# A VectorE loop and a finer up projection in a cached-attention decode kernel

## The chip, the cores and the metric

The kernel runs on one core of a Trainium2 chip, as one launch. The metric is the device time of that launch in microseconds. Data lie in the chip's HBM (DRAM) before and after; five engines work on them in the core's SBUF and PSUM: TensorE (PE, matmuls into PSUM), VectorE (DVE), ScalarE (ACT), GpSimd (POOL) and SyncE (SP, here only an issuer of DMAs). Each engine has a program of its own, and semaphores order them.

## The reference

One token of each of 8 sequences goes through a gated mix of attention over a long cache and a two-layer MLP. The output is 8 x 1 x 576.

```python
# x: 8 x 1 x 576   k_cache, v_cache: 8 x 32 x 4096 x 128   (bfloat16)
g = sigmoid((x * gate_w).sum(-1, keepdims=True))

q = (x @ wq).reshape(B, 1, 32, 128).transpose(0, 2, 1, 3)
scores = einsum("bhqd,bhkd->bhqk", q, k_cache) * 128 ** -0.5
o = einsum("bhqk,bhkd->bhqd", softmax(scores), v_cache)
a = o.transpose(0, 2, 1, 3).reshape(B, 1, 4096) @ wo

h = gelu(einsum("bsd,df->bsf", layernorm(x), w1) + b1)   # 576 -> 4608
b = einsum("bsf,fd->bsd", h, w2) + b2                    # 4608 -> 576

out = g * a + (1 - g) * b
```

The two caches hold 537 MB, the four weight matrices some 20 MB.

## The kernel before, in words

**Groups.** The attention is cut into 32 groups (`NG`), each of 8 heads (`HB`) of one sequence: `n = 8 * hg + b`. A group's cache is spread over 128 partitions, 16 partitions to a head and 256 keys (`NTT`) to a partition. Its keys come as two halves of 4 MiB into `KB[0]` and `KB[1]`, its values as 8 MiB into `VB`. All three buffers are single: a key half of the next group is loaded when the last multiply has read the old half, the next values when the last P·V matmul has read `VB`.

**One group.** `scores(n)` goes through 8 chunks (`NC`) of 32 keys. In `mult`, VectorE multiplies a chunk with the query (line 413, into one of two halves of `p1`), and TensorE sums groups of eight of the 128 products with an identity as held weights (lines 424 and 169, eight matmuls). In `reduce` (L431) VectorE adds the remaining 16. `softmax(n)` takes the maximum by transposes (L448 to L456), ScalarE does Exp (L457), and VectorE spreads the weights into `P` (L460) and sums them (L463, L464). `total` (L481) sums over partitions, `pv` does 64 matmuls of `P` with `VB` (L474), `evict` copies the result by ScalarE (L486), `gather` (L491) brings the heads together, and `norm` of group n, which stands in group n+1's program behind chunk 1, divides (L497, L498) and writes a column of `OT_sb`. The query is read from `q_bc`, which holds it for all groups, broadcast over partitions (L405).

**Loads.** All large loads are issued by SP in program order (helper lines L283 for keys, L288 for values, L250 for the rest) and share one hardware queue: for each group its two key halves and then its values, each held by a wait for its buffer. The buffer `RB` holds wq, then w1, then w2, then wo; each is loaded when the last matmul on the one before is done.

**The MLP between the groups.** `between(c)` is called behind each chunk and adds other work there. The up projection is 36 blocks of 6 matmuls (`up_proj`, L511), the activation is `act_h`, the down projection 36 blocks of 4 matmuls (`down_proj`, L536). Before, with `u` the key half that is being read:

```python
UP0, UPN = 3, 3          # up projection in key halves 3, 4, 5 (groups 1, 2, 2), 12 blocks in each
DN = 4                   # down projection in group 4
AP = 30                  # output projection of head group hg, from group 30 on
L0, L1 = 5, 29           # the loop's groups: 5 to 28
```

`load_w2` and `load_b2` (four small loads on ScalarE's queue) stand behind group 2, `load_wo` behind group 4.

**Programs.** `Stream` records the operations of each engine with their waits and numbers those that someone waits for. TensorE's program has a loop: `S.marks` holds where each of its groups 5 to 28 begins, and `emit_loop` writes one turn, in which a semaphore is awaited against a register that holds `turn * step + base` (L127). The other four engines' programs are straight code for all groups. A turn can be written once only if all its operations have the same operands in every group; VectorE's did not, since it read the query of group n from a place in `q_bc` and wrote a column of `OT_sb` that both depend on n.

**The end.** Groups 30 and 31 are in straight code in all programs. The last group's values come in parts (`V_LAST`), partly into `KB[0]`, its P·V is done the other way round (`pv_turned`), and `a_proj` and the last sum end the kernel.

Of the kernel before, what the change touches and what calls it, by code (L numbers as in the profile page):

```python
# [20 lines left out]
NJ = F // 128  # L21
# [20 lines left out]
class Stream:  # L42


    def __init__(self, nc):
        self.nc = nc
        self.ops = {e: [] for e in ("sync", "gpsimd", "scalar", "vector", "tensor")}
        self.sem = {e: nc.alloc_semaphore(f"sem_{e}") for e in ("gpsimd", "scalar", "vector", "tensor")}
        self.count = {e: 0 for e in self.sem}
        self.marks = []  # L50

    def op(self, engine, fn, waits=(), dma=None):

# [6 lines left out]
    def resolve(self):  # L60
        used = set()
        for ops in self.ops.values():
            for rec in ops:
                for w in rec[1]:
                    if w[0] == "op":
                        used.add(id(w[2]))
        for e, ops in self.ops.items():
            for rec in ops:
                if id(rec) in used:
                    self.count[e] += 1  # L70
                    rec[2] = self.count[e]
# [24 lines left out]

    def emit_loop(self, engine, eng, seen):

        turns = [self.ops[engine][a:b] for a, b in zip(self.marks[:-1], self.marks[1:])]
        assert len({len(t) for t in turns}) == 1  # L100
        step, waits = {}, []
        for recs in zip(*turns):
            assert len({(r[2] is None, r[3] is None) for r in recs}) == 1
            needs = [self.needs(r) for r in recs]
            assert len({frozenset(n) for n in needs}) == 1
            kept = []
            for key, (sem, val) in needs[0].items():
                vals = [n[key][1] for n in needs]
                d = vals[1] - vals[0]
                assert all(b - a == d for a, b in zip(vals[:-1], vals[1:]))  # L110
                if d == 0:
                    assert seen.get(key, 0) >= val
                    continue
                assert d > 0 and step.setdefault(key, d) == d
                kept.append((key, sem, val))
            waits.append(kept)
        base = {}
        for kept in waits:
            for key, sem, val in kept:
                base[key] = min(base.get(key, val), val)  # L120
        with eng.bass.Fori(0, len(turns), engines=OrderedEngineSet([eng.engine]), head_slot={eng.engine: 0}) as k:
            at = {key: eng.snap(k * step[key] + base[key]) for key in base}
            had = {}
            for rec, kept in zip(turns[0], waits):
                for key, sem, val in kept:
                    if had.get(key, 0) < val:
                        eng.wait_ge(sem, at[key] + (val - base[key]))  # L127
                        had[key] = val
                self.put(engine, eng, rec)
        for key, val in had.items():  # L130
            seen[key] = max(seen.get(key, 0), val + step[key] * (len(turns) - 1))


def bass_gated_mix__mha_block_cached__mixer_channel_mlp__decode_kernel(
# [20 lines left out]
    def pstride(t):  # L155
        return t[tuple([slice(None)] * len(t.shape))].ap[0][0]
# [71 lines left out]
    E = sb("E", [128, NTT], BF16)  # L228
    P = sb("P", [128, NTQ, HB, TQ], BF16)
    es = sb("es", [128, 1], F32)  # L230
    rs = sb("rs", [128, HB], F32)
    O_sb = sb("O_sb", [128, TQ, DH], F32)
    rz = sb("rz", [128, HB], F32)
# [165 lines left out]
    def q_of(b):  # L399
# [4 lines left out]
                start=True, stop=True), [*a_Q, c_Sel, a_qb.get(b - 1)] if i == 0 else ())  # L404
        a_qb[b] = op("scalar", lambda e: e.activation(out=q_bc[:, b, :], in_=qb_ps[:, :], func=ACT.Copy), [t])  # L405

    def mult(n, c):
        hg, b = divmod(n, B)
        u, par = n * NKH + c // NCK, c % 2
        t0 = (c % NCK) * CT  # L410
        qb = bass.AP(tensor=q_bc, offset=q_bc[:, b, hg * DH:(hg + 1) * DH].offset,
                     ap=[[pstride(q_bc), 128], [0, CT], [1, DH]])
        v_mult[n, c] = op("vector", lambda e: e.tensor_tensor(  # L413
            out=p1[:, par, :, :], in0=KB[u % NKH][:, t0:t0 + CT, :], in1=qb, op=ALU.mult),
            [k_land[u], a_qb[b], p_sum.get((n, c - 2) if c >= 2 else (n - 1, c + NC - 2))]
            + ([v_yT, p_yT, p_Q] if n == 0 and c < 2 else []))
        if c % NCK == NCK - 1:
            k_done[u] = v_mult[n, c]
        for i in range(NCH):
            r = bass.AP(tensor=p1, offset=p1[:, par, 0, i * CH:i * CH + 1].offset,  # L420
                        ap=[[pstride(p1), 128], [DH, CT], [1, CH]])
            w = [v_mult[n, c], v_red.get((n, c - 2) if c >= 2 else (n - 1, c + NC - 2)), *a_Q] if i == 0 else ()
            if i == 0:
                fn = lambda e, r=r: e.matmul(tr_ps[par][:, :], lhsT=ident[:, :], rhs=r, start=True, stop=False)  # L424
            else:
                fn = lambda e, r=r, i=i: held(e, tr_ps[par][:, :], ident[:, :], r, i == NCH - 1)
            p_sum[n, c] = op("tensor", fn, w)
# [65 lines left out]
                [a_ev[n], v_norm.get(n - 1), c_selO] if tt == 0 else ())  # L493

    def norm(n):
        hg, b = divmod(n, B)
        t = op("vector", lambda e: e.reciprocal(out=rz[:, :], in_=oz_ps[:, HB:2 * HB]), [p_oz[n]])  # L497
        v_norm[n] = op("vector", lambda e: e.tensor_tensor(  # L498
            out=OT_sb[:, hg * HB:(hg + 1) * HB, b], in0=oz_ps[:, 0:HB], in1=rz[:, :], op=ALU.mult), [t])


    st = {}
# [59 lines left out]
    def a_proj(hg):  # L562
        for h in range(hg * HB, (hg + 1) * HB):
            st["p_a"] = quarters(OT_sb[:, h, :], wo_sb[:, h, :], h == 0, h == H - 1,
                                 [v_norm[hg * B + B - 1], st["ld_wo"], st["v_bx"]] if h == hg * HB else ())


    def pv_turned(n, parts):
# [14 lines left out]
            [p_oz[n], v_rz[n]])  # L583


    UP0, UPN = 3, 3
    DN = 4
    AP = 30
    L0, L1 = 5, 29
    done_a = [0]  # L590
    last = NG - 1
    q_of(0)
    for n in range(NG):
        if L0 <= n <= L1:
            S.marks.append(len(S.ops["tensor"]))

        def between(c, n=n):
            u = n * NKH + c // NCK
            c4 = c % NCK
            if c == 1 and 1 <= n < last:  # L600
                norm(n - 1)
            if n == last and c == NCK:
                load_v_part(n, KB[0], 0, 0, NTK, [k_done[NKH * n]])
                t0 = NTK
                for nt in V_LAST:
                    load_v_part(n, VB, t0 - NTK, t0, t0 + nt, [p_pv[n - 1]])
                    t0 += nt
            if c4 == 2:
                if UP0 <= u < UP0 + UPN:
                    up_proj((u - UP0) * NJ // UPN, (u - UP0 + 1) * NJ // UPN)  # L610
                if n == DN:
                    down_proj((c // NCK) * NJ // 2, (c // NCK + 1) * NJ // 2)
                if n >= AP and done_a[0] < NHG - 1:
                    a_proj(done_a[0])
                    done_a[0] += 1
            if c4 == 3:
                if u == UP0 + UPN - 1:
                    act_h()
                if n == DN and c > NCK:
                    b_out()  # L620
            if n == 0 and c + 1 < B:
                q_of(c + 1)

        scores(n, between)
        softmax(n)
        if n < last:
            total(n)
        if n < last - 1:
            load_k(NKH * (n + 1))
            load_k(NKH * (n + 1) + 1)  # L630
            pv(n, (0,))
            evict(n)
            gather(n)
            if n + 1 < last - 1:
                load_v(n + 1)
        if n == last - 2:
            load_v_part(last - 1, VB, 0, 0, NTK, [v_done[n]])
        if n == last - 1:
            load_k(NKH * last)
            load_k(NKH * last + 1)  # L640
            load_v_part(n, VB, NTK, NTK, NTT, [v_done[n - 1]])
            pv(n, (0,))
        if n * NKH <= UP0 + UPN - 1 <= n * NKH + 1:
            load_w2()
            load_b2()
        if n == DN:
            load_wo()
# [19 lines left out]

    S.resolve()

    def tensor(eng):  # L670
        seen = {}
        S.emit("tensor", eng, seen, 0, S.marks[0])
        S.emit_loop("tensor", eng, seen)
        S.emit("tensor", eng, seen, S.marks[-1])

    with nc.Block() as block:
        for name in ("sync", "gpsimd", "scalar", "vector"):
            getattr(block, name)(lambda eng, name=name: S.emit(name, eng, {}))
        block.tensor(tensor)


# [26 lines left out]
```

## Time and profile before

| | |
|---|---|
| time, median of 3 runs | 1315.97 us (1313.71 to 1316.01) |
| the profiled execution's own time | 1315.18 us |
| its span, first to last instruction | 1313.4 us |
| mean granted TensorE clock | 0.838 |
| VectorE busy | 856.8 us (65%) |
| TensorE busy | 815.9 us (62%) |
| ScalarE busy | 47.9 us (4%) |
| read from HBM | 556.96 MB, 424 GB/s over the span |
| share of the 16 DMA engines' span, data queue q1 | 98.7% |
| chain that ended last | DMA 64%, VectorE 21%, TensorE 13% |

Views used below: the page (its lines on rates, queues and DMA issues), the chain of waits in order of time (start, length, what), the timeline of single engines (start, length, engine, line, operation, and in brackets the idle time before it with what ended it), and windows (busy time of each engine in a stretch, then the granted clock, the DMA engines' mean busy share and GB/s; a share can come out above 1 in a short window). A queue's row gives kind, packets, MB and the time of its packets as a share of 16 engines' span.

### The profile page before, as it was taken

To read this page: it belongs to the slowest core of one execution; us is meant where nothing else is said; L and a number is where in the kernel's file an instruction comes from. 1 tells how busy PE (TensorE), PEld (TensorE's weight loads), DVE (VectorE), ACT (ScalarE), POOL (GpSimd) and SP (SyncE) were. 2 spreads that over 40 slices of the span, in tenths; PEclk is the share of its full clock that TensorE was granted. 3 is DMA by queue.
4 is the path that set the end of the run, shared out by engine and by line. 5 is a ranking of instruction groups with operands and counts; after the bars stand their busy time and mean duration, and the time that the engine had idled before them with its cause. 6 is when DMAs were issued, how large, how long until landed. Compare 5 with 4: busy or idle time off the path is not lost.

```text
span 1313.4 us, 10207 instructions
## 1 busy us (share of the span) xinstructions
PE 815.9 (62%) x5156; PEld 170.7 (13%) x3364; DVE 856.8 (65%) x1094; ACT 47.9 (4%) x81; POOL 1.6 (0%) x12
## 2 busy tenths in 40 slices
PE   3647765655666666666565666565666666666666
PEld 0103311110111100111110111110111110011113
DVE  4565574556666677666677666668665667766685
ACT  1100000000000000000000000000000000000000
POOL 0000000000000000000000000000000000000000
PEclk8867797887887888787888878888977888878788
DMA  9999989999999999999999999999999999999997
GB/s 400 426 437 442 392 357 442 432 408 446 423 441 418 432 431 432 442 431 439 420 431 434 443 425 439 420 433 433 433 444 423 439 422 431 433 444 428 425 403 292
DMA packets 20904, 557.28 MB, mean 424 GB/s; under 512 B 2048, under 2 KB 6160, under 8 KB 7056
## 3 DMA queue, kind: packets, MB, share of 16 engines
q1 hardware_dynamic: 20624, 556.95, 98.7%
q8 instruction: 13, 0.21, 0.1%
q14 instruction: 11, 0.09, 0.0%
q10 hardware_dynamic: 256, 0.03, 0.0%
HBM read 556.96 MB, written 0.01 MB: 424 GB/s over the span
## 4 chain that ended last, share of the span: by engine, by line
DMA 64%; DVE 21%; PE 13%; issue 0%; SPq 0%; ACT 0%
DMA KB<-in_A_k_cache_dram 63%; DVE p L413 17%; PE psb L169 8%; DVE s_sb L431 4%; DMA VB<-in_A_v_cache_dram 2%; PE psb L424 2%; PE psb L511 1%; PE psb L474 1%; SPq L250 0%; DVE P L460 0%; PE psb L491 0%; PE psb L481 0%; ACT E L457 0%; DVE mA L448 0%; ACT O_sb L486 0%
## 5 line engine op out<-in xcount | busy, mean ns | idle before, releaser
L413 DVE TENSOR_TENSOR p<-KB,q_bc 128x4096 bf16<-128x4096 bf16 x256 | 581.9, 2283 | 310.3 <-DMA KB<-in_A_k_cache_dram 310.3
L169 PE MATMUL psb<-p,ident 128*128 128x512 bf16 x1792 | 487.8, 418 | 0.0
L424 PE MATMUL psb<-p,ident 128*128 128x512 bf16 x256 | 111.6, 436 | 299.2 <-DVE p L413 298.8
L431 DVE TENSOR_REDUCE s_sb<-psb 128x32 f32<-128x512 f32 x256 | 175.6, 686 | 91.8 <-PE psb L169 91.6
L474 PE MATMUL psb<-VB,P 128*32 128x512 bf16 x1984 | 176.5, 534 | 0.3 <-DMA VB<-in_A_v_cache_dram 0.2
L424 PEld LDWEIGHTS psb<-p,ident 128*128 128x128 bf16 x256 | 26.4, 103 | 738.9 <-DVE p L413 651.2
L481 PE MATMUL psb<-rs,ones 128*128 128x8 f32 x64 | 18.8, 367 | 155.5 <-DVE rs L464 154.9
L474 PEld LDWEIGHTS psb<-VB,P 128*32 128x32 bf16 x1984 | 64.5, 129 | 98.7 <-issue 83.1
L460 DVE TENSOR_SCALAR P<-E,own 128x256 bf16<-128x256 bf16 x248 | 51.5, 283 | 17.9 <-ACT E L457 17.9
L457 ACT ACTIVATE E<-s_sb,mD 128x256 bf16<-128x256 f32 x32 | 16.2, 507 | 919.5 <-DVE mD L456 919.5
L491 PE MATMUL psb<-selO,O_sb 128*128 128x8 f32 x248 | 33.6, 262 | 21.2 <-ACT O_sb L486 21.2
L481 PEld LDWEIGHTS psb<-rs,ones 128*128 128x128 f32 x64 | 15.8, 307 | 214.9 <-DVE rs L464 214.3
L491 PEld LDWEIGHTS psb<-selO,O_sb 128*128 128x128 f32 x248 | 30.8, 195 | 36.1 <-ACT O_sb L486 36.1
L486 ACT ACTIVATE O_sb<-psb 128x512 f32<-128x512 f32 x31 | 18.5, 596 | 259.0 <-PE psb L474 259.0
L511 PE MATMUL psb<-yT_sb,RB 128*128 128x8 bf16 (+1 forms) x216 | 19.6, 229 | 0.0
L511 PEld LDWEIGHTS psb<-yT_sb,RB 128*128 128x128 bf16 (+1 forms) x216 | 18.6, 165 | 5.7 <-issue 4.3
L448 DVE TENSOR_REDUCE mA<-s_sb 128x1 f32<-128x256 f32 x32 | 13.4, 420 | 1.1
L497 DVE RECIPROCAL rz<-psb 128x8 f32<-128x8 f32 x31 | 6.3, 202 | 11.3 <-PE psb L491 11.3
L463 DVE TENSOR_REDUCE es<-E 128x1 f32<-128x256 bf16 x32 | 13.2, 413 | 0.0
L387 PE MATMUL psb<-RB,p 128*8 128x512 bf16 x40 | 5.6, 626 | 5.3 <-DMA RB<-in_A_wq_dram 5.3
L464 DVE TENSOR_SCALAR rs<-own,es 128x8 f32<-128x8 f32 x32 | 7.4, 231 | 1.1
L456 DVE STREAM_TRANSPOSE mD<-mC 128x32 f32<-128x32 f32 x32 | 6.8, 212 | 1.1
(69 smaller groups left out, 86.2 us busy)
## 6 DMA issues: line engine op xcount, KB each, us to landing
KB<-in_A_k_cache_dram SPq DMA_DIRECT2D x64, 4096.0 KB, 26.9
VB<-in_A_v_cache_dram SPq DMA_DIRECT2D x2, 4096.0 KB, 24.0
RB<-in_B_w_dram SPq DMA_DIRECT2D x1, 5184.0 KB, 33.8
RB<-in_B_w_dram SPq DMA_DIRECT2D x1, 4608.0 KB, 45.6
RB<-in_A_wo_dram SPq DMA_DIRECT2D x1, 4608.0 KB, 45.3
RB<-in_A_wq_dram SPq DMA_DIRECT2D x1, 4096.0 KB, 12.4
KB<-in_A_v_cache_dram SPq DMA_DIRECT2D x1, 4096.0 KB, 17.8
VB<-in_A_v_cache_dram SPq DMA_DIRECT2D x2, 1024.0 KB, 21.0
```

The costliest lines, as they stand in the source:

```text
L169: return e.add_instruction(mybir.InstMatmult(name=nc.get_next_instruction_name(), engine=mybir.EngineType.PE, ins=[e.lower_ap(rhs), e.lowe ...
L413: v_mult[n, c] = op("vector", lambda e: e.tensor_tensor(out=p1[:, par, :, :], in0=KB[u % NKH][:, t0:t0 + CT, :], in1=qb, op=ALU.mult), [k_ ...
L424: fn = lambda e, r=r: e.matmul(tr_ps[par][:, :], lhsT=ident[:, :], rhs=r, start=True, stop=False)
L431: v_red[n, c] = op("vector", lambda e: e.tensor_reduce(out=s_sb[:, c * CT:(c + 1) * CT], in_=tr_ps[par][:, :].rearrange("p (t c) -> p t c" ...
L448: t = op("vector", lambda e: e.tensor_reduce(out=mA[:, 0:1], in_=s_sb[:, :], axis=AX.X, op=ALU.max), [v_red[n, NC - 1], c_mA])
L457: a_exp[n] = op("scalar", lambda e: e.activation(out=E[:, :], in_=s_sb[:, :], func=ACT.Exp, bias=mD[:, 0:1], scale=1.0), [v_nm[n], v_P.get ...
L460: v_P[n] = op("vector", lambda e, h=h: e.tensor_scalar(out=(P if n < NG - 1 else P_last)[:, :, h, :], in0=E[:, :].rearrange("p (q t) -> p ...
L474: p_pv[n] = op("tensor", lambda e, o=o, tq=tq, at=at, buf=buf: e.matmul(o, lhsT=P[:, tq, :, :].rearrange("p h t -> p (h t)"), rhs=buf[:, a ...
L481: p_z[n] = op("tensor", lambda e: e.matmul(oz_ps[:, HB:2 * HB], lhsT=ones[:, :], rhs=rs[:, :], start=True, stop=True), [v_rs[n], v_norm.ge ...
L486: a_ev[n] = op("scalar", lambda e: e.activation(out=O_sb[:].rearrange("p t d -> p (t d)"), in_=o_ps[0][:, :], func=ACT.Copy), [p_pv[n], p_ ...
L491: p_oz[n] = op("tensor", lambda e, tt=tt: e.matmul(oz_ps[:, 0:HB], lhsT=O_sb[:, tt, :], rhs=selO[:, tt, :], start=(tt == 0), stop=(tt == T ...
L511: st["p_up"] = op("tensor", lambda e, w=w, o=o, kt=kt: e.matmul(o, lhsT=w, rhs=yT_sb[:, kt, :], start=(kt == 0), stop=(kt >= NKF)), [*ld_w ...
```

## The change

VectorE's program of groups 6 to 29 becomes a loop, as TensorE's is. For that a group's query is copied by ScalarE to a fixed place, `q_n`, and its output is written to a fixed place, `O_n`, from which ScalarE copies it into `OT_sb`. The loop of both engines now covers groups 6 to 29; marks are held per engine, operations at the same place of a turn all signal if one of them does, and the first turn may wait for more than it needs. The up projection is cut into 12 pieces of 3 blocks, behind the odd chunks of groups 1, 2 and 3; activation, w2's load, down projection (now in 4 pieces) and wo's load come one group or two later: `act_h` in group 4, w2's load behind group 3, the down projection in group 5, wo's load behind it.

```diff
+    q_n = sb("q_n", [128, DH], BF16)
+    O_n = sb("O_n", [128, HB], BF16)
...
+    def q_group(n):
+        hg, b = divmod(n, B)
+        a_q[n] = op("scalar", lambda e: e.activation(out=q_n[:, :], in_=q_bc[:, b, hg * DH:(hg + 1) * DH], func=ACT.Copy),
+                    [a_qb[b], v_mult.get((n - 1, NC - 1))])
+
+    def put(n):
+        hg, b = divmod(n, B)
+        a_O[n] = op("scalar", lambda e: e.activation(
+            out=OT_sb[:, hg * HB:(hg + 1) * HB, b], in_=O_n[:, :], func=ACT.Copy), [v_norm[n]])
 
     def mult(n, c):
...
-            [k_land[u], a_qb[b], p_sum.get((n, c - 2) if c >= 2 else (n - 1, c + NC - 2))]
+            [k_land[u], a_q[n], p_sum.get((n, c - 2) if c >= 2 else (n - 1, c + NC - 2))]
...
     def norm(n):
         t = op("vector", lambda e: e.reciprocal(out=rz[:, :], in_=oz_ps[:, HB:2 * HB]), [p_oz[n]])
         v_norm[n] = op("vector", lambda e: e.tensor_tensor(
-            out=OT_sb[:, hg * HB:(hg + 1) * HB, b], in0=oz_ps[:, 0:HB], in1=rz[:, :], op=ALU.mult), [t])
+            out=O_n[:, :], in0=oz_ps[:, 0:HB], in1=rz[:, :], op=ALU.mult), [t, a_O.get(n - 1)])
+        put(n)
...
-    UP0, UPN = 3, 3
-    DN = 4
+    UP, NUP = 1, 3
+    DN = UP + NUP + 1
     AP = 30
-    L0, L1 = 5, 29
+    L0, L1 = DN + 1, 30
...
     q_of(0)
+    q_group(0)
     for n in range(NG):
         if L0 <= n <= L1:
-            S.marks.append(len(S.ops["tensor"]))
+            for e in ("tensor", "vector"):
+                S.marks.setdefault(e, []).append(len(S.ops[e]))
...
-            if c4 == 2:
-                if UP0 <= u < UP0 + UPN:
-                    up_proj((u - UP0) * NJ // UPN, (u - UP0 + 1) * NJ // UPN)
-                if n == DN:
-                    down_proj((c // NCK) * NJ // 2, (c // NCK + 1) * NJ // 2)
...
+            if c % 2 == 1 and UP <= n < UP + NUP:
+                i = (n - UP) * NC // 2 + c // 2
+                up_proj(i * NJ * 2 // (NUP * NC), (i + 1) * NJ * 2 // (NUP * NC))
+            if n == UP + NUP and c == 3:
+                act_h()
+            if n == DN and c % 2 == 0:
+                down_proj(c * NJ // NC, (c + 2) * NJ // NC)
+            if n == DN and c == NC - 1:
+                b_out()
...
         scores(n, between)
+        if n < last:
+            q_group(n + 1)
         softmax(n)
...
-        if n * NKH <= UP0 + UPN - 1 <= n * NKH + 1:
+        if n == UP + NUP - 1:
             load_w2()
             load_b2()
```

More of the change, by code (lines that the diff above doesn't have):

```diff
@@ L49, in __init__ @@
         self.count = {e: 0 for e in self.sem}
-        self.marks = []
+        self.marks = {}
     def op(self, engine, fn, waits=(), dma=None):
@@ L66, in resolve @@
                         used.add(id(w[2]))
+        for e, marks in self.marks.items():
+            for recs in zip(*(self.ops[e][a:b] for a, b in zip(marks[:-1], marks[1:]))):
+                if any(id(r) in used for r in recs):
+                    used.update(id(r) for r in recs)
         for e, ops in self.ops.items():
@@ L97, in emit_loop @@
     def emit_loop(self, engine, eng, seen):
-        turns = [self.ops[engine][a:b] for a, b in zip(self.marks[:-1], self.marks[1:])]
+        turns = [self.ops[engine][a:b] for a, b in zip(self.marks[engine][:-1], self.marks[engine][1:])]
         assert len({len(t) for t in turns}) == 1
@@ L108, in emit_loop @@
                 vals = [n[key][1] for n in needs]
-                d = vals[1] - vals[0]
-                assert all(b - a == d for a, b in zip(vals[:-1], vals[1:]))
+                d = vals[2] - vals[1]
+                val = vals[1] - d
+                assert vals[0] <= val and all(b - a == d for a, b in zip(vals[1:-1], vals[2:]))
                 if d == 0:
@@ L405, in q_of @@
         a_qb[b] = op("scalar", lambda e: e.activation(out=q_bc[:, b, :], in_=qb_ps[:, :], func=ACT.Copy), [t])
+    a_q, a_O = {}, {}
+    def q_group(n):
[6 more added lines that the diff above has]
+            out=OT_sb[:, hg * HB:(hg + 1) * HB, b], in_=O_n[:, :], func=ACT.Copy), [v_norm[n]])
     def mult(n, c):
-        hg, b = divmod(n, B)
         u, par = n * NKH + c // NCK, c % 2
         t0 = (c % NCK) * CT
-        qb = bass.AP(tensor=q_bc, offset=q_bc[:, b, hg * DH:(hg + 1) * DH].offset,
-                     ap=[[pstride(q_bc), 128], [0, CT], [1, DH]])
+        qb = bass.AP(tensor=q_n, offset=0, ap=[[pstride(q_n), 128], [0, CT], [1, DH]])
         v_mult[n, c] = op("vector", lambda e: e.tensor_tensor(
             out=p1[:, par, :, :], in0=KB[u % NKH][:, t0:t0 + CT, :], in1=qb, op=ALU.mult),
-            [k_land[u], a_qb[b], p_sum.get((n, c - 2) if c >= 2 else (n - 1, c + NC - 2))]
+            [k_land[u], a_q[n], p_sum.get((n, c - 2) if c >= 2 else (n - 1, c + NC - 2))]
             + ([v_yT, p_yT, p_Q] if n == 0 and c < 2 else []))
@@ L495, in norm @@
     def norm(n):
-        hg, b = divmod(n, B)
         t = op("vector", lambda e: e.reciprocal(out=rz[:, :], in_=oz_ps[:, HB:2 * HB]), [p_oz[n]])
         v_norm[n] = op("vector", lambda e: e.tensor_tensor(
-            out=OT_sb[:, hg * HB:(hg + 1) * HB, b], in0=oz_ps[:, 0:HB], in1=rz[:, :], op=ALU.mult), [t])
+            out=O_n[:, :], in0=oz_ps[:, 0:HB], in1=rz[:, :], op=ALU.mult), [t, a_O.get(n - 1)])
+        put(n)
     st = {}
@@ L564, in a_proj @@
             st["p_a"] = quarters(OT_sb[:, h, :], wo_sb[:, h, :], h == 0, h == H - 1,
-                                 [v_norm[hg * B + B - 1], st["ld_wo"], st["v_bx"]] if h == hg * HB else ())
+                                 [a_O.get(min(hg * B + B - 1, NG - 2)), v_norm.get(NG - 1), st["ld_wo"], st["v_bx"]] if h == hg * HB else ())
     def pv_turned(n, parts):
@@ L592, in bass_gated_mix__mha_block_cached__mixer_channel_mlp__decode_kernel @@
     q_of(0)
+    q_group(0)
     for n in range(NG):
         if L0 <= n <= L1:
-            S.marks.append(len(S.ops["tensor"]))
+            for e in ("tensor", "vector"):
+                S.marks.setdefault(e, []).append(len(S.ops[e]))
         def between(c, n=n):
-            u = n * NKH + c // NCK
-            c4 = c % NCK
             if c == 1 and 1 <= n < last:
@@ L607, in between @@
                     t0 += nt
-            if c4 == 2:
-                if UP0 <= u < UP0 + UPN:
-                    up_proj((u - UP0) * NJ // UPN, (u - UP0 + 1) * NJ // UPN)
-                if n == DN:
-                    down_proj((c // NCK) * NJ // 2, (c // NCK + 1) * NJ // 2)
[L613 to L620, printed above, removed]
+            if c % 2 == 1 and UP <= n < UP + NUP:
[7 more added lines that the diff above has]
+                b_out()
+            if n >= AP and c % NCK == 2 and done_a[0] < NHG - 1:
+                a_proj(done_a[0])
+                done_a[0] += 1
             if n == 0 and c + 1 < B:
@@ L668, in bass_gated_mix__mha_block_cached__mixer_channel_mlp__decode_kernel, with program @@
     S.resolve()
[L670 to L674, printed above, removed]
+    def program(name, eng):
+        seen, marks = {}, S.marks.get(name)
+        S.emit(name, eng, seen, 0, marks and marks[0])
+        if marks:
+            S.emit_loop(name, eng, seen)
+            S.emit(name, eng, seen, marks[-1])
     with nc.Block() as block:
-        for name in ("sync", "gpsimd", "scalar", "vector"):
-            getattr(block, name)(lambda eng, name=name: S.emit(name, eng, {}))
-        block.tensor(tensor)
+        for name in ("sync", "gpsimd", "scalar", "vector", "tensor"):
+            getattr(block, name)(lambda eng, name=name: program(name, eng))
 _INS = ['A_x', 'A_k_cache', 'A_v_cache', 'A_wq', 'A_wo', 'B_x', 'B_w1', 'B_b1', 'B_w2', 'B_b2', 'gate_w']
```

## The prediction

> **What bounds the kernel now.** I read the page first, then the chain of waits in order of time, the SP queue's timeline, and windows where the pace breaks.
>
> ```profile
> GB/s 400 426 437 442 392 357 442 432 408 446 423 441 418 432 431 432 442 431 439 420 431 434 443 425 439 420 433 433 433 444 423 439 422 431 433 444 428 425 403 292
> q1 hardware_dynamic: 20624, 556.95, 98.7%
> q8 instruction: 13, 0.21, 0.1%
> q14 instruction: 11, 0.09, 0.0%
> RB<-in_B_w_dram SPq DMA_DIRECT2D x1, 5184.0 KB, 33.8
> RB<-in_A_wo_dram SPq DMA_DIRECT2D x1, 4608.0 KB, 45.3
> ```
>
> The data queue q1 takes 98.7% of the 16 DMA engines' time, so compute matters only where it lets that queue run empty. The rate dips in slices 5 and 6 (392, 357) and at the end. q8 and q14 carry nothing but instructions.
>
> In the chain, each of these rows is the first multiply of a group, which waits for the group's keys (start, length):
>
> ```profile
> 77.43 2.30 DVE p L413
> ...
> 212.59 2.31 DVE p L413
> ...
> 252.81 2.30 DVE p L413
> ...
> 303.72 2.30 DVE p L413
> ...
> 458.88 2.30 DVE p L413
> ...
> 497.66 2.30 DVE p L413
> ...
> 537.42 2.30 DVE p L413
> ...
> 1239.36 2.30 DVE p L413
> ```
>
> They start groups 1, 4, 5, 6, 10, 11, 12 and 30. Group 10 takes 497.66 - 458.88 = 38.78 us for its 16 MiB, which is 432.6 GB/s. Group 11 takes 39.76, that is 0.98 more. Two stretches are slower than this pace.
>
> Head, groups 1 to 5: 303.72 - 77.43 = 226.29 us. Five groups (193.90), w2 (5184 KB, 12.27) and wo (4608 KB, 10.91) at 432.6 GB/s make 217.08. So 9.2 us are lost.
>
> Middle, groups 6 to 29: 1239.36 - 303.72 = 935.64 against 24 x 38.78 = 930.72. So 4.92 us are lost, five times 0.98; by the same view's other starts the five are groups 11, 15, 19, 23 and 27.
>
> Where the head loses (window, length, busy time of PE, PEld, DVE, ACT, POOL, clock, DMA share, GB/s):
>
> ```profile
> 150.00:162.00 12.00, 7.00 (x47) 3.29 (x40) 7.03 (x23) 2.23 (x3) 0.00 (x0) 0.67 1.02 437
> 162.00:172.00 10.00, 9.29 (x83) 3.71 (x76) 4.63 (x4) 0.60 (x1) 0.00 (x0) 0.72 0.34 123
> ```
>
> From 162 to 172 the DMA engines are idle for 0.66 x 10 = 6.6 us. The SP queue and then the chain say why:
>
> ```profile
> 168.65 0.33 SPq L288 DMA_DIRECT2D VB<-in_A_v_cache_dram  x1
> ...
> 534.06 0.33 SPq L288 DMA_DIRECT2D VB<-in_A_v_cache_dram  x1
> ```
> ```profile
> 99.60 6.40 PE psb L511 x72
> ...
> 129.42 6.34 PE psb L511 x72
> ...
> 146.97 6.39 PE psb L511 x72
> ```
>
> Group 3's values are issued only at 168.65, when group 2's last P·V matmul frees VB, and everything queued before them had landed. Group 2 carries two of the three up-projection pieces. In a steady group the values are issued at 534.06 while the first key half ahead of them lands at 537.42 and the second half one (9.7 us) later: 13 us to spare.
>
> **Part 1, the up projection.** The same 216 matmuls (19.1 us, 0.089 each) become four pieces of 18 (1.6 us) in each of groups 1, 2 and 3, behind the sums of the odd chunks. Between two chunks TensorE waits for the next product:
>
> ```profile
> 512.19 0.39 PE L424 MATMUL psb<-p,ident 128*128 128x512 bf16 x1 [0.90 <-DVE p L413]
> ```
>
> So 0.9 us of a piece is covered and 0.7 is not; three pieces cost a group 2.1 us, and the fourth, behind the last chunk, lies under the softmax. Group 2 loses 6.34 + 6.39 and gets 2.1, so its P·V ends 10.6 us earlier, at 158, ahead of 162. With every piece uncovered (6.6 us a group) it ends at 162.5, just as the queue runs out; what I leave out, the activation that moves from group 2 to group 4, is on the safe side. Group 3 gets 2.1 to 6.6 against the 13 us that a steady group has to spare. The queue does not run dry.
>
> w2 is requested after group 3 and wo after group 5. Each still stands behind one group's keys and values and ahead of the next; that moves their 23.2 us without adding. The SP queue's waits for them are on matmuls that ended earlier, so no key load behind them is held. b2's four small loads move with w2, on ScalarE's queue behind group 3's eviction. The down projection's four pieces of 36 fall in group 5 and are covered likewise.
>
> Gain: 6.6 us of idle, and part of the other 2.6. Group 4 took 252.81 - 212.59 - 38.78 = 1.44 too much, where no load but its own ran; its window holds instruction packets:
>
> ```profile
> q8 instruction: 2, 0.03, 0.3%
> q14 instruction: 1, 0.01, 0.0%
> ```
>
> Below I argue that such a packet sets back one DMA engine. The dry stretch had levelled the engines and these packets set some back again; without it the set-back of the first groups just stays. I take 7.6 (ends 5 and 8.1).
>
> **Part 2, VectorE's loop.** What are the five times 0.98? The first row is q14 over groups 6 to 28 (260 to 1200 us), the second over group 11 alone; the third counts VectorE's instructions in group 10 (x34):
>
> ```profile
> q14 instruction: 8, 0.07, 0.0%
> ```
> ```profile
> q14 instruction: 1, 0.01, 0.1%
> ```
> ```profile
> 458.88:497.66 38.78, 23.19 (x138) 4.18 (x82) 26.42 (x34) 1.10 (x2) 0.00 (x0) 0.91 1.00 433
> ```
>
> q8 does not appear in those 940 us at all, in which TensorE's program is already a loop. What is left on q14 is straight code. A packet has some 8 KB (0.07 MB in 8). Four groups of 34 VectorE instructions would fill one at 60 B each, and every fourth group is long. My reading: such a packet delays one and the same DMA engine by 0.98 us, a key load ends only when its last engine does, and nothing lets that engine catch up. The end of the run agrees, where its work is last:
>
> ```profile
> 1304.00:1308.00 4.00, 3.47 (x115) 3.44 (x114) 0.61 (x3) 0.00 (x0) 0.00 (x0) 0.50 0.09 33
> ```
>
> A share of 0.09 is one to two engines of 16 still moving for 4 us when the rest are done: about the 4.92. Against it: group 10 has a q14 packet too and is not long. It could be ScalarE's or SP's, on an engine that is ahead.
>
> The Trainium skill, "Runtime: NRT & Kernel Launch", section "Instruction fetch mechanics", calls the cost of a new block of instructions mostly hidden and prefers unrolled code. By that the 0.98 has another cause and this part saves nothing; the sum would be rival B's. The long groups speak against it, but no run here has separated the two yet.
>
> A looped body asks for no new packets while it stays in the instruction memory, as TensorE's does. Entering it can ask for one or two (0.98 each), since its head is put on a boundary. I take 4.9 - 1.3 = 3.6 (ends 0 and 4.9).
>
> What the loop adds: register operations, one for nearly every wait, about 25 a turn, at TensorE's price,
>
> ```profile
> L127 PEldq ALU_OP  x216: 32/32/42, 255.2 to 1195.5; - x108
> L405 ACT ACTIVATE q_bc<-psb 128x512 bf16<-128x512 f32 x8 | 4.8, 597 | 21.6 <-PE psb L401 21.6
> ```
>
> so 0.8 us, with a branch of unknown length. VectorE is idle 38.78 - 26.42 = 12.4 us of a group, and the 13 us to spare cover several more. The two ScalarE copies cost at most 0.6 us each (second row, four times the columns). q's copy follows the previous group's last multiply, seven us of softmax ahead of its reader; the output's copy is read by the last stage alone. Ahead of Exp and eviction they queue only when their input has long arrived. If that cover were gone, a group would lengthen by up to 1.2 us, 29 in all.
>
> **Sum.** The profiled execution took 1315.18 us (span 1313.4 and 1.8 around it). Minus 7.6 and 3.6 it is 1304.0. The median of the runs, 1315.97, is 0.8 higher, so I forecast 1304.8.
>
> **Rivals.**
>
> A, the forecast: 1304.8. With both gains whole it is 1315.97 - 8.1 - 4.9 = 1303.0; with 6 and 2 in place of 7.6 and 3.6, near 1308.
>
> B, only the head gains: the long groups come from something else with a period of four, or the loop's entry puts as many packets on the late engine as it saves. 1315.97 - 7.6 = 1308.4. For it: group 10's packet without effect.
>
> C, only the loop gains: the dry stretch moves to group 3 or 4 as TensorE, at half clock (0.50 after 162), needs longer for pieces than I allow. 1315.97 - 3.6 = 1312.4. Against it: group 2 would have to lose 10 us again.
>
> D, slower: VectorE's loop fetches its body anew each turn. Every turn then sets the same engine back 0.98: 24 x 0.98 = 23.5 in place of 4.9, so 18.6 more, minus 7.6 of the head: 1327.0. It decides from 13 packets in 24 turns on (12.5 / 0.98). For it: VectorE's packets are 8 KB where q8's are 16 (0.21 MB in 13), so it holds less code at a time. Against it: 34 instructions and 25 register operations are half of an 8 KB packet, and TensorE's longer body causes no fetch. The same section of the Trainium skill says that a taken branch to a block that is no longer held must wait for its fetch; the trace has no such branch to test that.
>
> **How the numbers follow.** A 0.70, B 0.11, C 0.08, D 0.08; 0.03 for the rest, two thirds of it within 0.2% (2.6 us, about what a measurement of this kernel can tell from no change). Faster: A, B, C and 0.01 are 0.90; same 0.02; slower 0.08. The range takes A and B: from 1301.5 (1303.0 less 1.5 for the scatter of the runs, 1313.71 to 1316.01) to 1309.0 (B and 0.6). C and D stay outside.
>
> **What would show it.** Right: no window of DMA share below 0.9 between 80 and 260 us; group starts at an even 38.78 from group 6 to 30 with few or no q14 packets between; group 6 starting near 296 and group 30 near 1228; the DMA share dropping on all engines together at the end. Wrong: q14 counting 20 or more packets, long groups still every fourth, a new dry stretch in groups 3 to 5, or VectorE's chain (not the key loads) between two group starts.

## The result, and the profile after

The changed kernel takes 1305.3 us (median of 6 runs, 1304.64 to 1305.71), the kernel before 1315.49 in the same series (1313.71 to 1316.01). The ratio is 0.9924, 95% interval 0.9911 to 0.9937: 10.2 us less. The forecast was 1304.8, 11.2 less. The profiled execution after took 1304.64 us, with a span of 1302.8. One execution of the kernel before, in a later series, took 2928.99 us; it is left out, and the median of that series is over the other six.

From the page after: rates in the 40 slices, and the queues.

```profile
GB/s 401 417 451 425 440 419 427 441 431 410 442 431 431 424 433 434 443 435 433 424 433 431 440 433 435 432 428 432 433 440 429 434 428 433 434 442 429 423 432 304
q1 hardware_dynamic: 20624, 556.95, 99.4%
q8 instruction: 13, 0.21, 0.1%
q14 instruction: 7, 0.06, 0.0%
```

The dip in slices 5 and 6 (392, 357) is gone (440, 419). q1 moves the same bytes in the same packets and now takes 99.4% of the engines' time. q14 has 7 packets in place of 11.

The stretch that was dry, after (window, length, busy time of PE, PEld, DVE, ACT, POOL, clock, DMA share, GB/s), and the issue of group 3's values on the SP queue:

```profile
162.00:172.00 10.00, 8.91 (x63) 3.49 (x39) 10.00 (x8) 0.00 (x0) 0.00 (x0) 1.00 1.01 436
```
```profile
151.44 0.33 SPq L295 DMA_DIRECT2D VB<-in_A_v_cache_dram  x1
```

The share was 0.34 and is 1.01. The values are issued at 151.44, not 168.65, 17.2 us earlier and well ahead of 162.

The chain after, the first multiplies of groups 1, 4, 5, 6, 7 and 30 (start, length):

```profile
77.16 2.30 DVE p L430
...
193.62 2.30 DVE p L430
...
245.26 2.30 DVE p L430
...
286.22 2.30 DVE p L430
...
337.07 2.30 DVE p L430
...
1228.83 2.30 DVE p L430
```

wo's load now stands between groups 6 and 7 in this list, not between 5 and 6, so from here on I compare at group 7. Before, its first multiply began at 342.50 in the chain; now it begins at 337.07, so 5.4 us are gained by then. From group 7 to 30 there are 23 groups, 23 x 38.78 = 891.9. After takes 1228.83 - 337.07 = 891.76: no long group is left. Before took 1239.36 - 342.50 = 896.86, which is 5.1 more. The two gains make 10.5 at group 30, close to the 10.54 between the two profiled executions' own times (1315.18 and 1304.64); the stretch from there to the end of the span lasts as long as it did (74.0 us in both).

The packets of q14 over groups 7 to 29 (window 345 to 1225), after; the same window of before has 8. A row of q14 does not say which engine's code it carries:

```profile
q14 instruction: 1, 0.01, 0.0%
```

Two things in the new profile did not look as foretold. The first is the entry into VectorE's loop: its branch and its first register operation (line, engine, operation, count: shortest/median/longest ns, first to last start).

```profile
L126 DVEq COMPARE_BRANCH  x25: 50/56/63, 275.1 to 1220.0; - x25
L126 DVEq FUSED_REGOPS  x24: 62/63/63, 280.7 to 1181.1; - x24
```

The first branch is at 275.1 and the loop's first operation at 280.7, 5.6 us later. In that time the DMA queues of the window 275 to 290 carry

```profile
q8 instruction: 1, 0.02, 0.4%
q14 instruction: 2, 0.02, 0.3%
```

The second is the end. In the window where the last data land, the share does not fall at once on all engines:

```profile
1294.00:1298.00 4.00, 3.49 (x129) 3.35 (x129) 0.23 (x2) 0.00 (x0) 0.00 (x0) 0.50 0.16 60
```

So some engines still come in late.

### The profile page after: what moved, and what is told of

Its sections match the earlier page's. It is cut to its first block, busy times and chain, and to the rows that moved or that the text cites. A ratio compares the mean times of both kernels' runs of the same rounds, so it can differ in the third digit from the quotient of the medians.

```text
span 1302.8 us, 10855 instructions
## 1 busy us (share of the span) xinstructions
PE 812.6 (62%) x5156; PEld 171.6 (13%) x3364; DVE 855.5 (66%) x1094; ACT 65.1 (5%) x144; POOL 1.6 (0%) x12
## 3 DMA queue, kind: packets, MB, share of 16 engines
q1 hardware_dynamic: 20624, 556.95, 99.4%
## 4 chain that ended last, share of the span: by engine, by line
DMA 69%; DVE 18%; PE 9%; issue 3%; SPq 0%; DVEq 0%; ACT 0%
DMA KB<-in_A_k_cache_dram 67%; DVE p L430 16%; PE psb L174 7%; DVE s_sb L448 2%; DMA VB<-in_A_v_cache_dram 2%; PE psb L441 1%; SPq L257 0%; PE psb L491 0%; DVEq L132 0%; PE psb L553 0%; DVE P L477 0%; PE psb L498 0%; ACT E L474 0%; DVE mA L465 0%; PE psb L589 0%
## 5 line engine op out<-in xcount | busy, mean ns | idle before, releaser
L430 DVE TENSOR_TENSOR p<-KB,q_n 128x4096 bf16<-128x4096 bf16 x256 | 581.5, 2282 | 322.7 <-DMA KB<-in_A_k_cache_dram 313.6
L418 ACT ACTIVATE q_n<-q_bc 128x128 bf16<-128x128 bf16 x32 | 9.9, 309 | 528.8 <-DVE p L430 528.8
L423 ACT ACTIVATE OT_sb<-O_n 128x8 bf16<-128x8 bf16 x31 | 7.4, 237 | 252.2 <-DVE O_n L514 252.2
```

The lines of the kernel that those rows point to most:

```text
L430: v_mult[n, c] = op("vector", lambda e: e.tensor_tensor(out=p1[:, par, :, :], in0=KB[u % NKH][:, t0:t0 + CT, :], in1=qb, op=ALU.mult), [k_ ...
```

## The experiments

Two theories of the middle were set against each other. S, the prediction's: each packet of VectorE's code that is fetched sets one DMA engine back by about 0.98 us for good. P: the long groups have another cause with a period of four groups. For the head, the question was how much the spreading of the up projection does by itself; for the loop, where its entry is paid and whether its body is fetched again.

### One part of the change at a time

**The loop alone** is the changed kernel with the up projection, activation, down projection and loads where they were before:

```diff
-    UP, NUP = 1, 3
-    DN = UP + NUP + 1
+    UP0, UPN = 3, 3
+    DN = 4
...
-    L0, L1 = DN + 1, 30
+    L0, L1 = 6, 30
```

> The kernel after, with the up projection, activation, down projection and the loads of w2 and wo put back where they stood before (three pieces in groups 1, 2, 2); VectorE's loop over groups 6 to 29 and ScalarE's two copies stay. Theory S (each packet of VectorE's code sets one DMA engine back by 0.98 us for good): the dry stretch of some 6.6 us around 162 to 172 us stays, five long groups (4.9 us) go and two packets at the loop's entry come (2.0 us), so about 2.9 us below before: 1312.6. Theory P (the long groups have another cause with a period of four, all of the gain is the head's): 1315.5, with long groups still every fourth.

Measured: 1310.97 us (1310.07 to 1312.18) against 1314.93 before, ratio 0.9971 (0.9961 to 0.9981), 4.0 us less. Its dry stretch is there, somewhat shorter than before (share 0.50 against 0.34); its starts of groups 5, 7 and 30 come from the chain, its q14 packets are those of the window 345 to 1225:

```profile
162.00:172.00 10.00, 9.29 (x86) 3.07 (x66) 4.77 (x6) 0.83 (x2) 0.00 (x0) 0.79 0.50 182
```
```profile
251.78 2.30 DVE p L430
...
342.90 2.30 DVE p L430
...
1234.80 2.30 DVE p L430
```
```profile
q14 instruction: 1, 0.01, 0.0%
```

Group 5 starts 1.0 earlier than before (251.78 against 252.81) and group 7 starts 0.4 later (342.90 against 342.50): some 1.4 us are lost where the loop is entered. Then come 891.90 us for the 23 groups: the loop removes the long groups. Theory S gave 1312.6 and P 1315.5; the run is 1.6 below S, of which the shorter dry stretch accounts for some 1.0. The long groups went with the packets.

**The pieces alone** is the changed kernel with VectorE's program straight:

```diff
-            for e in ("tensor", "vector"):
+            for e in ("tensor",):
```

> The kernel after, with VectorE's program straight for all groups; TensorE's loop, the two copies by ScalarE and the 12 pieces of the up projection stay. Theory S: no dry stretch, 7.4 us below before at the end of the head, and five or six long groups of 39.76 us again among groups 6 to 29: about 1308 (before less 7.4). Theory P: no long groups lost or won by the loop, so the same as after, 1305.3.

Measured: 1308.41 us (1308.31 to 1308.65) against 1314.93, ratio 0.9952 (0.9936 to 0.9969), 6.5 us less. The chain's starts of groups 7, 11, 12 and 30, and the q14 packets from 345 to 1225:

```profile
335.80 2.30 DVE p L430
...
490.90 2.30 DVE p L430
...
530.54 2.30 DVE p L430
...
1232.46 2.30 DVE p L430
```
```profile
q14 instruction: 7, 0.06, 0.0%
```

Group 11 is long again (530.54 - 490.90 = 39.64, 0.86 more than 38.78), and the 23 groups take 896.66, 4.7 too much. The ScalarE copies are in this kernel as well, so it is not they that removed the long groups in the kernel after. P's value was 1305.3, S's 1308.

### More code, nothing else

The kernel before with 32 tiny VectorE instructions behind the softmax of each of the groups 6 to 29, where VectorE is idle:

```diff
+    more = sb("more", [128, 32], F32)
...
+        if 6 <= n < 30:
+            for i in range(32):
+                memset("vector", more[:, i:i + 1], 0.0)
```

> The kernel before, with 32 more tiny VectorE instructions (a memset of one column of a scratch tile) behind the softmax of each of groups 6 to 29; they change no result and take some 2 to 3 us of a group in which VectorE is idle for 12. Theory S: 66 instructions a group fill a packet in about two groups, so 12 or 13 packets in place of 6 set the engine back: long groups about every second, 6 to 7 us above before, 1322. Theory P: the period of the long groups does not depend on VectorE's code, 1315.5 and every fourth group long.

Measured: 1320.66 us (1319.81 to 1320.75) against 1314.93, ratio 1.0046 (1.0029 to 1.0062), 5.7 us more. Its row among the groups of instructions, its q14 packets from 345 to 1225, and the starts of groups 7 and 30 on VectorE's timeline:

```profile
L307 DVE MEMSET more<- 128x1 f32 x768 | 12.0, 59 | 1.1 <-issue 0.4
```
```profile
q14 instruction: 13, 0.11, 0.0%
```
```profile
340.74 2.29 DVE L414 TENSOR_TENSOR p<-KB,q_bc 128x4096 bf16<-128x4096 bf16 x1 [8.83 <-DMA KB<-in_A_k_cache_dram]
...
1243.28 2.29 DVE L414 TENSOR_TENSOR p<-KB,q_bc 128x4096 bf16<-128x4096 bf16 x1 [8.80 <-DMA KB<-in_A_k_cache_dram]
```

The added instructions are 59 ns each, 1.9 us a group, and both first multiplies still waited nearly 9 us for their keys: VectorE's work does not bound. Yet the 23 groups take 902.54, that is 10.6 above 891.94, and by the chain's other starts every second group is long, 11 of them, by 0.96 on average. Twice the code made twice the long groups. This is the strongest of the three results for S, whose 1322 came within 1.4 us: P, and any cause in VectorE's busy time, gave no change.

### Where the loop's entry is paid

**Head of the loop elsewhere.** A loop's first instruction can be put at a chosen place (`head_slot`, counted in instructions) within a block of 256. I take that as two stretches of 128, each of which at the 60 B of the prediction is about one 8 KB packet; the change puts the head at 0, the start of such a stretch.

```diff
-        with eng.bass.Fori(..., head_slot={eng.engine: 0}) as k:
+        with eng.bass.Fori(..., head_slot={eng.engine: 64 if engine == "vector" else 0}) as k:
```

> The kernel after, with VectorE's loop head put on slot 64 of a 256-instruction block in place of slot 0; some 300 instructions stand ahead of the loop, so it should begin in the block that is already held and end ahead of its half. Theory S: the two packets at 278.7 and 284.5 us and the 11 us wait at the entry go; the late engine is 2 us less late, but the next engine is only 1.1 us behind it, so 1.1 us below after: about 1304.2. Theory P, and the view that the entry costs nothing because the keys are not there yet: 1305.3.

Measured: 1302.93 us (1302.73 to 1303.58), ratio to before 0.9912 (0.9896 to 0.9929). Its branch and first loop operation, the starts of groups 6, 7 and 30 in the chain, and the queues from 275 to 290:

```profile
L126 DVEq COMPARE_BRANCH  x25: 50/56/63, 274.6 to 1219.1; - x25
L126 DVEq FUSED_REGOPS  x24: 62/63/63, 274.8 to 1180.5; - x24
```
```profile
284.10 2.30 DVE p L430
...
336.24 2.30 DVE p L430
...
1228.00 2.30 DVE p L430
```
```profile
q1 hardware_dynamic: 207, 6.26, 97.1%
q8 instruction: 1, 0.02, 0.5%
```

The loop begins 0.2 us after its branch, not 5.6, and no q14 packet is fetched there. Group 6 starts 2.1 us earlier than in the kernel after, group 30 0.8 earlier. S's 1304.2 was 1.3 too high. The 1.1 us by which it had the late engine behind the next one stand in no row.

The kernel after and this one once more, next to each other with five rounds:

> The kernel after once more, on the same chip as the next one. If the two packets at the loop's entry cost what theory S says, it stays 1 to 2.5 us above the next; if the difference seen so far (1305.3 against 1302.9) was that between chips, the two agree within 0.5 us. Two or more q14 packets between 275 and 290 us.

> The kernel with the loop's head on slot 64 once more, on the same chip as the one before. Theory S: 1 to 2.5 us below it, no q14 packet between 275 and 290 us, and the second latest DMA engine shows in the tail. Otherwise: the same within 0.5 us.

Measured: 1305.33 (1304.37 to 1305.53) and 1302.99 (1302.72 to 1303.98), ratios to before 0.9928 (0.9914 to 0.9941) and 0.9914 (0.9901 to 0.9928). No run of the one lies in the range of the other; the difference is 2.3 us. The head at 64 is 11.5 us below before, and no other version is faster.

Not all of the 2.3 us is the entry's. At group 30 the two kernels are 0.8 us apart in the first pair of profiles (1228.83 and 1228.00) and 1.0 in the second (1228.73 and 1227.73). The rest lies behind VectorE's last operation. In the chains of before, of the kernel after and of the head at 64 it is

```profile
1310.68 0.37 DVE out_sb L660
```
```profile
1299.06 0.37 DVE out_sb L678
```
```profile
1298.25 0.37 DVE out_sb L678
```

The spans end at 1313.4, 1302.8 and 1300.9, that is 2.7, 3.7 and 2.7 us later. From 1299 to 1302.8 the kernel after has

```profile
q14 instruction: 1, 0.01, 0.5%
```

and the other two have no q14 packet behind this operation. All eleven profiles agree: the four with such a packet (the kernel after, its repeat, the loop alone, one piece a group; all with a VectorE loop whose head is at 0) end 3.6 to 3.9 us after the operation's start, the seven without it 2.6 to 2.8. So the place of the head seems to move a fetch at the end of the program too, worth about 1 us; no run sets that apart.

**Is the body fetched again?** With the head at 100 the body, shorter than 128 instructions, crosses from one such stretch into the next, so every turn runs in both and branches back across the boundary.

```diff
+        with eng.bass.Fori(..., head_slot={eng.engine: 100 if engine == "vector" else 0}) as k:
```

> The kernel after, with VectorE's loop head on slot 100 of its block, so that the 56 instructions of a turn lie across a boundary of 128 instructions (one packet of 8 KB). Theory H (two neighbouring packets are both held and the branch back finds its target): no packets in the loop, 1303 to 1306. Theory D (rival D's mechanism: the code behind the boundary pushes the loop's head out, and each turn fetches it anew): at least one packet a turn, 24 x 0.98 = 23.5 us on the one late engine, 1327 or more, 1350 with two a turn, and a wait of VectorE's for code in each turn.

Measured: 1302.98 us (1302.63 to 1303.61) against 1314.92, ratio 0.9913 (0.9895 to 0.993). From 345 to 1225:

```profile
q14 instruction: 1, 0.01, 0.0%
```

23 of the 24 turns, one packet: both stretches are held, and nothing is fetched again turn by turn. Rival D, 1327.0, would need one a turn.

### The up projection in one piece a group

The changed kernel, each third of the up projection in one piece of 72 matmuls behind chunk 6 of groups 1, 2 and 3:

```diff
-            if c % 2 == 1 and UP <= n < UP + NUP:
-                i = (n - UP) * NC // 2 + c // 2
-                up_proj(i * NJ * 2 // (NUP * NC), (i + 1) * NJ * 2 // (NUP * NC))
+            if c == 6 and UP <= n < UP + NUP:
+                up_proj((n - UP) * NJ // NUP, (n - UP + 1) * NJ // NUP)
```

> The kernel after, with the up projection uncut: one piece of 72 matmuls (6.4 us) behind chunk 6 in each of groups 1, 2 and 3. It tells cutting from spreading. Theory spread (one piece a group and the activation in group 4 are enough for group 2's P.V to end before the queue is empty): 1305 to 1306, group starts of groups 3 and 4 within 0.5 us of after. Theory cut (only small pieces are covered by TensorE's waits): group 2's P.V ends 4 to 6 us later than in after, the queue runs dry again for a part of the 6.6 us, 1307 to 1310.

Measured: 1307.41 us (1305.89 to 1309.06) against 1314.92, ratio 0.9948 (0.993 to 0.9966), 7.5 us less. The window and the issue of group 3's values:

```profile
162.00:172.00 10.00, 7.41 (x34) 0.35 (x5) 8.46 (x8) 0.24 (x1) 0.00 (x0) 1.00 1.01 436
```
```profile
160.42 0.33 SPq L295 DMA_DIRECT2D VB<-in_A_v_cache_dram  x1
```

The values are issued at 160.42, just ahead of 162, and the queue does not run dry. That group 2 has one piece rather than two, with the activation moved out of it, is thus enough to fill the dry stretch. The finer cut moves the issue a further 9 us forward, which is worth some 2 us in the median. Neither theory holds whole: the queue does not run dry, as spread has it, but the time lies in the range of cut. In the profiled executions 0.9 of it is there at groups 7 and 30 (337.94 and 1229.70 against 337.07 and 1228.83) and 1.7 at the end (spans of 1304.5 and 1302.8). As no queue is empty in that stretch, the mechanism of these 2 us is open, and four runs that scatter over 3 us size it badly.

### The copies on another engine

In the kernel with the head at 64, both copies by GpSimd in place of ScalarE:

```diff
-        a_q[n] = op("scalar", lambda e: e.activation(out=q_n[:, :], in_=..., func=ACT.Copy),
+        a_q[n] = op("gpsimd", lambda e: e.tensor_copy(out=q_n[:, :], in_=...),
...
-        a_O[n] = op("scalar", lambda e: e.activation(out=..., in_=O_n[:, :], func=ACT.Copy), [v_norm[n]])
+        a_O[n] = op("gpsimd", lambda e: e.tensor_copy(out=..., in_=O_n[:, :]), [v_norm[n]])
```

> The kernel with the loop's head on slot 64 (1302.9), with both copies of a group made by GpSimd in place of ScalarE. ScalarE's program gets shorter again, so its packet at 310.7 us, in whose group the key load came 1.3 us later than wo explains, should move to about 490 us, where before had it without effect. Theory S: 1301.6 to 1302.9, if GpSimd's own packets do not fall on the late engine. If the copies or their waits matter in themselves (a copy of 0.3 us becomes one of 1 us or more): no change all the same, since VectorE waits for keys for 8 us in each group; a slower VectorE beside GpSimd would show as longer multiplies, not as time.

Measured: 1303.33 us (1302.71 to 1303.84) against 1314.92, ratio 0.9913 (0.9895 to 0.9931): no difference from the head at 64 on ScalarE. The copies' rows among the groups of instructions, first of the kernel after, then of this one:

```profile
L418 ACT ACTIVATE q_n<-q_bc 128x128 bf16<-128x128 bf16 x32 | 9.9, 309 | 528.8 <-DVE p L430 528.8
L423 ACT ACTIVATE OT_sb<-O_n 128x8 bf16<-128x8 bf16 x31 | 7.4, 237 | 252.2 <-DVE O_n L514 252.2
```
```profile
L418 POOL COPY q_n<-q_bc 128x128 bf16<-128x128 bf16 x32 | 9.3, 289 | 582.8 <-DVE p L430 537.6 <-ACT q_bc L412 45.2
L423 POOL COPY OT_sb<-O_n 128x8 bf16<-128x8 bf16 x31 | 6.8, 218 | 692.6 <-DVE O_n L514 692.6
```

The copies are covered on either engine. The run was made to catch a fetch of ScalarE's code in group 6. That fetch moved from 310.7 to 482.6 us as meant, but group 6 with wo's load stayed as long (335.85 - 284.20 = 51.65, against 52.14), so that packet is not why this stretch is longer than its bytes. At its new place, in group 10, it cost nothing either: that group took 38.78.

## Why the prediction was right, point by point

**The bound.** Right. Nothing that was added to VectorE (register operations, 32 extra instructions a group) or taken from ScalarE moved the time by its own duration; time moved where data stopped or code was fetched.

**Part 1, the head.** The mechanism was right, and the late issue of group 3's values was the cause of the dry stretch. Two sizes were off. The pieces were charged 2.1 us to a group; group 2's P·V was to end at 158, and its successor's values were issued at 151.44. The pieces cost next to nothing: the multiplies of group 2 from 121.79 to 136.00 follow each other 2.8 to 3.0 us apart with or without a piece between them. And group 1's old piece had not been counted. It had pushed group 1's P·V past the start of group 2 at 116.21, to 121.06; now it ends at 113.72 (the first row is from the chain before, the second from TensorE's timeline after):

```profile
115.12 5.94 PE psb L474 x64
```
```profile
107.95 5.77 PE L491 MATMUL psb<-VB,P 128*32 128x512 bf16 x64
```

This changed nothing in the sum, since 158 was early enough. The gain of 7.6 (ends 5 and 8.1) measured 6.7 at group 7 in the kernel with the pieces alone (342.50 - 335.80), 6.9 at group 30 (1239.36 - 1232.46) and 6.5 in its runs: the dry 6.6 us and little of the 1.44 that I had added in part. Group 4 was late by more than its own load in the new kernel too (245.26 - 193.62 = 51.64, less 38.78 and w2's 12.27 is 0.6), so a part of that was no gift of the dry stretch.

**Part 2, the loop.** The step that carried most risk, reading the five long groups as fetched code, held in three independent ways: they go with the packets (loop alone), they stay with them (pieces alone), they double with them (more code). Not every packet costs: before, group 7 (342.50 to 381.31) holds a q14 packet too and took 38.81; the pieces alone show the same. The place of this packet, four groups ahead of group 11, suggests that it is VectorE's, and why it cost nothing is open (by S, the engine that it met was not yet the late one). Group 10's packet, the doubt in the prediction, fits ScalarE's, which cost nothing in group 10 of the last run either. That the delay sits on one DMA engine is not shown by a row of that engine; it is still argued, from the share of 0.09 at the end of the kernel before. The kernel with more code does not help: if one engine were never to catch up, its 11 long groups would leave a tail twice as long. It is about as long as before's, with a share of 0.85 in the 4 us ahead of this window and 0.02 in the 6 us behind it:

```profile
1308.00:1312.00 4.00, 3.47 (x97) 3.38 (x98) 0.61 (x3) 0.00 (x0) 0.00 (x0) 0.50 0.09 34
```

The packets that made a group long cost 0.95 to 0.98 us each before and 0.96 on average with more code, in a kernel whose data queue takes 98.7% of the DMA engines' time. The Trainium skill, "Runtime: NRT & Kernel Launch", section "Instruction fetch mechanics", calls the cost of crossing into a new block mostly hidden. These groups do not agree with it.

The entry was sized about right: 1.3 us taken. The kernel after starts group 7 1.3 later than the pieces alone (337.07 and 335.80), and is 0.8 to 1.0 behind the head at 64 at group 30. I had counted the packets, but not that the branch to the loop waits for code, 5.6 us. In the chain that wait does not show: the first multiply, at 286.22, was released by the load of its keys. The Trainium skill states in the same section that a taken branch to a block outside the two that are held waits for its fetch. The 5.6 us agree with it, and so does the head at 100, whose branch back between two neighbouring stretches fetched nothing from 345 on. Without the entry the loop is worth 1308.41 - 1302.93 = 5.5 us in the runs, against 4.9; with it 1232.46 - 1228.83 = 3.6 at group 30, as forecast.

**The sum.** At group 30, 6.9 and 3.6 in place of 7.6 and 3.6, which is 10.5 in place of 11.2 (10.2 in the medians): the head's term was too large, and the time is within the range. That the end added nothing is luck. Counted from group 30, VectorE's last operation comes 1.1 us sooner than before (1299.06 - 1228.83 = 70.23 against 1310.68 - 1239.36 = 71.32), and the stretch behind it is 1.0 longer; the sum had neither.

**The rivals.** B (1308.4, head only) is refuted by the middle without long groups; its number is what the pieces alone measured. C (1312.4, loop only) by the share of 1.01. D (1327.0) by one packet in 23 groups, and by the head at 100.

**What would show it.** No share below 0.9 between 80 and 260: right, in windows of 20 us the lowest are

```profile
180.00:200.00 20.00, 13.01 (x94) 4.72 (x85) 8.71 (x21) 2.62 (x4) 0.00 (x0) 0.69 0.94 405
```

and one of 0.93 in 100 to 120. In windows of 10 us, 100 to 110 has 0.87, the same as before the change, and no other is below 0.9. Group 30 near 1228: right (1228.83). Group 6 near 296: wrong by 10 us (286.22), since I had counted wo's 10.91 ahead of it. The SP queue's timeline of the kernel after shows the order, keys of group 6 first, then that group's values, then wo:

```profile
257.17 11.53 SPq L290 DMA_DIRECT2D KB<-in_A_k_cache_dram  x2
281.33 0.33 SPq L295 DMA_DIRECT2D VB<-in_A_v_cache_dram  x1
281.70 0.44 SPq L257 DMA_DIRECT2D RB<-in_A_wo_dram  x1
```

So wo's load delays group 7's keys, not group 6's.

All engines finishing together: wrong. The entry's fetches are not the cause, since the head at 64, which has none, comes in no better:

```profile
1294.00:1298.00 4.00, 3.49 (x122) 3.23 (x119) 0.19 (x1) 0.00 (x0) 0.00 (x0) 0.50 0.16 59
```

What is the cause stays open. Nor is the stretch of group 6 with wo's load explained, which takes 1.2 us more than its bytes in the kernel after (50.85 - 38.78 - 10.91) and 2.5 with the head at 64; so 1.3 of the 2.1 us by which the entry delays group 6 come back in it.

## What to carry to other kernels

Where one DMA queue is busy 99% of the time, code is traffic too: count the instruction packets of every engine, look whether the loads that come late coincide with them, and make the longest straight program a loop, even if two small copies have to be added to give its operands fixed places. Choose where the loop's head lies, since an entry that jumped to a stretch not yet fetched waited and fetched at once here, and since the code behind the loop moves with it. Whether any of this pays where the queue is less full, no run shows. Work that one group does for another stage is best looked at by which buffer it keeps occupied: here it held a buffer of values, and moving a part of it out of one group filled a dry stretch of 6.6 us while TensorE's total work stayed the same.

## What the runs showed of the hardware

A packet of VectorE's code, 8 KB (0.11 MB in 13), cost this kernel, whose data queue takes 98.7% of the DMA engines' time, 0.95 to 0.98 us in each of five long groups before and 0.96 on average in eleven with more code, never regained within the 23 groups measured; the packet in group 7 cost nothing. TensorE's packets are of 16 KB (0.21 MB in 13). A jump into a loop whose code was not held took 5.6 us from the branch to the first operation; one whose code was held took 0.2. A loop placed across a boundary of 128 instructions ran 23 turns with one q14 packet. A q14 packet behind VectorE's last operation went with an end about 1 us later (four profiles against seven).
